# First 224 slots of expert 0 multiplied while the last tokens are routed, and a shorter routing in batches of 8, 7, 3, 3 and 3 rounds

## Chip, core and metric

The kernel runs on one core of one Trainium2 chip. TensorE (PE) multiplies, VectorE (DVE), ScalarE (ACT) and GpSimd (POOL) do the elementwise work, and SyncE (SP) issues most DMAs. The metric is the device time of one execution in microseconds, the median of several. All tensors in memory are float32.

## What is computed

Three blocks follow each other: a gated linear attention, a mixture of experts in which each token goes to one expert, and a gated two-matrix block.

```python
def _attn_ref(q, k, v, f_logit):            # (4, 8, 768, 48)
    f = 1.0 / (1.0 + np.exp(-f_logit))
    for t in range(S):
        state = f[:, :, t, :, None] * state + np.einsum('bhd,bhe->bhde', k[:, :, t], v[:, :, t])
        y[:, :, t] = np.einsum('bhd,bhde->bhe', q[:, :, t], state)

def _moe_ref(x, expert_emb, tau, w1, w2):   # x (3072, 384), 8 experts, w1 (8, 384, 1024)
    logits = xn @ en.T / tau                # xn, en: rows divided by norm + 1e-6
    expert_idx = np.argmax(logits, axis=1)
    probs = softmax(logits)
    for e in range(E):
        mask = expert_idx == e
        h = np.maximum(x[mask] @ w1[e], 0.0)
        out[mask] = probs[mask, e, None] * (h @ w2[e])

def _moe2_ref(x, w_a, w_b, w_out):          # 384 -> 1536 -> 384
    return ((x @ w_a) * (x @ w_b)) @ w_out
```

## The kernel before

**Attention.** 24 rounds `g`, each of 128 tokens of one batch entry and all heads. In a round DVE makes two scans for the decays (`scan_b` of round g+2 at line 190, `scan_r` at line 201) and the products around them, PE the scores, the products with v and the state, ACT the evacuations, POOL the scaled keys `kt` and one causal mask. `turn_y` gives the 128 tokens in PSUM as x together with their logits. Everything is recorded in a fixed order, and each engine works its queue in that order.

**Routing.** Rounds are routed in batches that end at the rounds in `ROUNDS`: 7, 6, 5, 4 and 2 rounds. `route` is a generator whose steps `tick` puts between the rounds: DVE finds each token's expert (`oh`), PE counts ranks (`rk`, on `ones` and `tri`), ACT makes a tanh, DVE the position `posi` and the gate. POOL makes the norm (`nrm`, line 360). `scatter_row` then sends one round's 128 rows by an indirect DMA of POOL to `slots` in memory, at expert times 3072 plus rank. A row is 4 words (token id, gate) and 384 values.

**Weights.** A piece is half of an expert's w1 or w2, 768 KB. It is loaded to one of two `raw` buffers (`w_load`, `job_load`), ACT copies the high part (`w_hi`, line 104, or line 707), and DVE and POOL subtract the low part (`w_lo`, line 112, or line 710). Each product is then three matmuls: high by high, low by high, high by low (`mm3`, lines 810 to 812). Pieces 0 and 1 are made during the attention, 2 and 3 behind the routing.

**Experts.** 64 steps `s`, eight for each expert. Each expert has 448 slots (`CAP`). `rows_load(e)` loads them, `rows_gate` scales them, `x_turn` transposes them and splits them. A step does nine matmuls of w1 (`h_part`), the relu and its split (`h_split`, lines 832 and 833), converts waiting pieces (`w_more`), and does nine matmuls of w2 for the step before (`y_part`, line 863). At expert 0 the rows of expert 2 are asked for in step 6 and scaled in step 8, ahead of the evacuation of expert 0's output on ACT (line 881). `w_more` converts pieces 4 and 5 in step 1 and pieces 6 and 7 in step 5; the loads of the next pieces are issued behind that, as the buffers come free. SP works its loads in order.

**Between the two.** After the last round the queue of DVE holds the rest of the routing, then some fifteen small instructions that make the offsets and a flag (lines 640 to 655; the flag chooses a slow general path when an expert got more than 448 or fewer than 256 tokens), and then the first work on expert 0's rows. PE runs 24 matmuls on zeros there (`warm_up`).

**Last block.** Six tiles of 512 tokens by 12 steps, whose output rows are sent by an indirect DMA.

Of the kernel before, what the change touches and what calls it, by code (L numbers as in the profile page):

```python
# [21 lines left out]
HP = 112  # L22
# [20 lines left out]
ROUNDS = (6, 12, 17, 21, 23)  # L43
C0 = 2.0 ** -15
NWARM3 = 24


def build(tc, I, out, dbg=None):
# [19 lines left out]
    idx = const.tile([128, NT // 128], I32, name="idx")  # L68

# [47 lines left out]
    with tc.manual_schedule():  # L117
# [5 lines left out]
        x_p = actx.enter_context(tc.tile_pool(name="x", bufs=3))  # L123
# [192 lines left out]
        def rounds():  # L316
            return dict(lg=r_p.tile([128, RB, NE], F32, tag="lg", name="lg"),
                        ssq=r_p.tile([128, RB], F32, tag="ssq", name="ssq"),
                        xb=x_p.tile([128, RB, RW], F32, tag="xb", name="xb"), n=0)
# [15 lines left out]
        def x_lg(g):  # L335
# [4 lines left out]
            if g in ROUNDS:  # L340
                bg.append(route(rd))

# [4 lines left out]
        def route(rd):  # L347
            nb = rd["n"]
            lg, ssq = rd["lg"][:, 0:nb], rd["ssq"][:, 0:nb]
            rt = lambda nm, w=NE, dt=F32: r_p.tile([128, RB, w], dt, tag=nm, name=nm)[:, 0:nb]  # L350
# [9 lines left out]
            G.tensor_tensor(out=nrm[:, :, 0], in0=ssq, in1=half[:, 0:nb], op=ALU.pow)  # L360
            yield
# [3 lines left out]
            eq = rt("eq")  # L365
            V.tensor_tensor(out=eq, in0=lg, in1=bc(mx), op=ALU.is_ge)
            yield
# [3 lines left out]
            V.tensor_tensor(out=eq, in0=eq, in1=prio_b, op=ALU.mult)  # L371
# [6 lines left out]
            yield  # L378
            V.tensor_scalar(out=nrm, in0=nrm, scalar1=1e-6, scalar2=None, op0=ALU.add)
# [10 lines left out]
            for i in range(nb - 1):  # L390
                T.matmul(out=ps[:, i + 1:nb], lhsT=ones,
                         rhs=oh[:, i:i + 1].to_broadcast([128, nb - 1 - i, NE]),
                         start=False, stop=(i == nb - 2), skip_group_check=True)
            A.activation(out=z, in_=z, func=ACTF.Tanh, scale=0.5)
            yield
# [4 lines left out]
            pos = rt("pos", 1)  # L400
            V.tensor_reduce(out=pos, in_=pz, axis=AX.X, op=ALU.add)
            yield
            posi = r_p.tile([128, RB, 1], I32, tag="posi", name="posi", bufs=4)[:, 0:nb]
            V.tensor_copy(posi, pos)
# [8 lines left out]
            gate = rt("gate", 1)  # L413
            V.tensor_reduce(out=gate, in_=den, axis=AX.X, op=ALU.add)
            yield
            V.tensor_scalar(out=gate, in0=gate, scalar1=1e-9, scalar2=None, op0=ALU.add)
            yield
            V.reciprocal(out=rd["xb"][:, 0:nb, 1:2], in_=gate)
# [10 lines left out]
        def scatter_row():  # L429
            if scaled:  # L430
# [6 lines left out]
                scat.append(sc)  # L437

# [107 lines left out]
        rd = rounds()  # L546
        for g in range(NG):
# [7 lines left out]
            if g in (2, 12, 14):  # L555
                w_load()
            scan_b(g + 2)
            scores(g + 1)
            tick(g > 5)
# [15 lines left out]
            evac_y(g)  # L575
            if g > 0:
                turn_y(g - 1)
            for _ in range(2 if g < NG - 2 else 6):
# [6 lines left out]
            if g > 0:  # L585
                x_copy(g - 1, rd)
# [10 lines left out]
            if g == NG - 1:  # L597
                w_lo(V, 1)
                w_load()
            tick(3 if g < 19 else 6)  # L600
# [12 lines left out]
        x_lg(NG - 2)  # L613
# [3 lines left out]
        finish()  # L617
        scatter_row()
        scatter_row()
        last = st[NG - 1]  # L620
        x_lg(NG - 1)
        tick()
        st[NG - 1] = last
        x_copy(NG - 1, dict(rd, n=rd["n"] - 1))
        flush_rows()
        finish()
        flush_rows()
# [7 lines left out]
        fl2 = ob_p.tile([1, 3], F32, name="fl2")  # L635
        pc = ps_r.tile([128, 2, 128], F32, tag="r", name="pc")
# [592 lines left out]
```

## Time and profile before

| | us |
|---|---|
| median of 3 runs (lowest, highest) | 888.29 (887.59, 888.86) |
| the profiled execution | 889.81 |
| its span, first to last instruction | 888.0 |
| TensorE busy in the span | 837.8 (94%) |
| VectorE busy | 426.0 (48%) |
| ScalarE busy | 352.9 (40%) |
| GpSimd busy | 245.4 (28%) |

The shares are averages over stages that differ: the attention up to about 147 us, the rest of the routing and the way to the first expert up to about 174 us, the experts up to about 410 us, and the last block. A term that depends on a stage is read from that stretch.

### The profile page before, as it was taken

The page shows a single profiled execution, that of the slowest core. Times are in us where ns is not written, and L with a number is a line of the kernel's source. Part 1 is how long each engine was busy: PE and PEld are TensorE (multiplying, and loading weights), DVE is VectorE, ACT ScalarE, POOL GpSimd, SP SyncE. Part 2 cuts the span into 40 slices and gives each one's busy share as a digit, 9 for nine tenths or more (in the row PEclk, how much of TensorE's full clock was granted, in tenths as well). Part 3 has the DMA queues.
Part 4 walks back from the last instruction along what each step waited for, and adds up shares of the span by engine and source line. Part 5 has one row for each costly group of instructions (what it writes and reads, how often), then busy time and mean ns, then how long its engine had stood idle before and what let it go on. Part 6 is the DMA issues. An engine that isn't in the chain of part 4 may idle for free. (4 is left out here: it accounts for less than half of the span.)

```text
span 888.0 us, 12718 instructions
## 1 busy us (share of the span) xinstructions
PE 837.8 (94%) x5027; PEld 735.4 (83%) x5028; DVE 426.0 (48%) x710; ACT 352.9 (40%) x663; POOL 245.4 (28%) x230
## 2 busy tenths in 40 slices
PE   6899885598999999999998999999999999999996
PEld 4788774397999999999887888888888888888885
DVE  8999996534354445438688423122221312222221
ACT  4798873254455545533444212122221212222111
POOL 6453767433543463441222010010010001001001
PEclk8899998699999999999999999999999999999998
DMA  9898843433634453452233000000000000000001
GB/s 194 193 218 206 224 113 126 157 103 102 198 125 142 165 173 108 140 177 72 72 111 104 1 36 1 1 36 1 0 36 1 1 1 36 0 1 36 1 1 38
DMA packets 36598, 76.58 MB, mean 86 GB/s; under 512 B 4492, under 2 KB 18660, under 8 KB 36532
## 3 DMA queue, kind: packets, MB, share of 16 engines
q1 hardware_dynamic: 33332, 65.91, 26.8%
q0 software_dynamic: 3072, 9.49, 2.9%
q8 instruction: 41, 0.67, 0.3%
q10 hardware_dynamic: 128, 0.30, 0.1%
q14 instruction: 25, 0.20, 0.1%
HBM read 63.79 MB, written 11.90 MB: 85 GB/s over the span
## 5 line engine op out<-in xcount | busy, mean ns | idle before, releaser
L811 PE MATMUL pa<-a,w 128*128 128x512 f32 (+1 forms) x438 | 170.8, 390 | 0.0
L812 PE MATMUL pa<-a,w 128*128 128x512 f32 (+1 forms) x438 | 170.8, 390 | 0.0
L810 PE MATMUL pa<-a,w 128*128 128x512 f32 (+1 forms) x438 | 169.5, 387 | 0.0
L966 DVE TENSOR_TENSOR rows<-rows,pa 128x512 f32<-128x512 f32 (+1 forms) x73 | 49.6, 680 | 242.6 <-PE pa L812 242.6
L993 POOL DMA_INDIRECT out<-yT,idx x24 | 23.4, 975 | 363.8 <-ACT yT L991 358.3
L962 ACT ACTIVATE rows<-pa 128x512 f32<-128x512 f32 (+1 forms) x73 | 43.1, 591 | 164.7 <-PE pa L812 164.4
L967 ACT ACTIVATE gh<-rows 128x512 fp32r<-128x512 f32 (+1 forms) x73 | 45.6, 625 | 143.9 <-DVE rows L966 143.9
L710 POOL TENSOR_TENSOR w<-raw,w 128x512 fp32r<-128x512 f32 x56 | 84.7, 1533 | 62.0 <-ACT w L707 62.0
L981 PE MATMUL pq<-w,gl 128*128 128x384 f32 x288 | 97.8, 340 | 2.1 <-DVE gl L968 2.0
L979 PE MATMUL pq<-w,gh 128*128 128x384 f32 x288 | 97.2, 338 | 1.2 <-ACT gh L967 1.2
L980 PE MATMUL pq<-w,gh 128*128 128x384 f32 x288 | 96.9, 337 | 0.0
L812 PEld LDWEIGHTS pa<-a,w 128*128 128x128 f32 x438 | 82.5, 188 | 16.9
L811 PEld LDWEIGHTS pa<-a,w 128*128 128x128 f32 x438 | 82.5, 188 | 15.4
L810 PEld LDWEIGHTS pa<-a,w 128*128 128x128 f32 x438 | 82.6, 189 | 15.2
L863 PE MATMUL po<-hh,w 128*128 128x448 f32 x384 | 91.4, 372 | 2.4 <-ACT yT L881 2.3
L968 DVE TENSOR_TENSOR gl<-rows,gh 128x512 fp32r<-128x512 f32 (+1 forms) x73 | 60.1, 823 | 52.1 <-ACT gh L967 52.1
L832 ACT ACTIVATE hh<-ph 128x448 fp32r<-128x448 f32 x64 | 34.9, 546 | 113.3 <-PE ph L812 113.3
L863 PEld LDWEIGHTS po<-hh,w 128*128 128x128 f32 x384 | 70.4, 188 | 9.2 <-ACT yT L881 2.9
L833 DVE SCALAR_TENSOR_TENSOR hl<-ph,hh 128x448 fp32r<-128x448 f32 x64 | 39.9, 623 | 79.0 <-ACT hh L832 78.7
L728 POOL TENSOR_TENSOR w<-raw,w 128x768 fp32r<-128x768 f32 x18 | 33.9, 1881 | 142.3 <-ACT w L727 142.3
L810 PE MATMUL ph<-a,w 128*128 128x448 f32 x192 | 71.5, 372 | 0.0
L811 PE MATMUL ph<-a,w 128*128 128x448 f32 x192 | 71.1, 371 | 0.0
(174 smaller groups left out, 1381.6 us busy)
## 6 DMA issues: line engine op xcount, KB each, us to landing
raw<-moe_w SPq DMA_DIRECT2D x32, 768.0 KB, 4.5
qkf<-qkf SPq DMA_DIRECT2D x44, 288.0 KB, 6.2
rows<-slots SPq DMA_DIRECT2D x7, 679.0 KB, 6.5
vx<-vx SPq DMA_DIRECT2D x24, 192.0 KB, 4.8
raw<-moe_w_a SPq DMA_DIRECT2D x6, 768.0 KB, 4.3
raw<-moe_w_b SPq DMA_DIRECT2D x6, 768.0 KB, 4.5
raw<-moe_w_out SPq DMA_DIRECT2D x6, 768.0 KB, 4.5
slots<-raw SPq DMA_DIRECT2D x8, 291.0 KB, 5.1
```

The lines of the kernel that those rows point to most:

```text
L710: (G if i < NPOOL else V).tensor_tensor(out=wt[:, 1, f], in0=raw[:, f], in1=wt[:, 0, f].bitcast(F32), op=ALU.subtract)
L810: T.matmul(out=out, lhsT=wh, rhs=xh, start=first, stop=False)
L811: T.matmul(out=out, lhsT=wl, rhs=xh, start=False, stop=False)
L812: T.matmul(out=out, lhsT=wh, rhs=xl, start=False, stop=last)
L863: T.matmul(out=OS[e][k], lhsT=w[:, j % 4, k * 128:(k + 1) * 128], rhs=x, start=(j == 0 and w is wh and x is hh), stop=(j == FJ - 1 and x i ...
L962: A.activation(out=ab[:, r], in_=pa, func=ACTF.Copy)
L966: V.tensor_tensor(out=ab[:, r], in0=ab[:, r], in1=pp[1], op=ALU.mult)
L967: A.activation(out=gh[:, r], in_=ab[:, r], func=ACTF.Copy)
L968: V.tensor_tensor(out=gl[:, r], in0=ab[:, r], in1=gh[:, r].bitcast(F32), op=ALU.subtract)
L979: T.matmul(out=q, lhsT=gh[:, c], rhs=wh[:, f % 4], start=(f == 0), stop=False)
L980: T.matmul(out=q, lhsT=gh[:, c], rhs=wl[:, f % 4], start=False, stop=False)
L981: T.matmul(out=q, lhsT=gl[:, c], rhs=wh[:, f % 4], start=False, stop=(f == F2J - 1))
```

## The change

Expert 0's first 224 slots (`EN`) are loaded once the first 18 rounds have been scattered, and multiplied through both weight matrices while the last rounds are routed; the 224 other slots follow afterwards in the old place, as steps of 224 columns. The batches of the routing are 8, 7, 3, 3 and 3 rounds, a batch takes 15 DVE instructions in place of 20, and the reciprocal of the gate is taken where the rows are read. Each batch's rows have a buffer of their own. Pieces 2 and 3 are loaded in rounds 13 and 19; piece 2 and two thirds of piece 1's low part go into the rounds, piece 3 behind them. The matmuls on zeros are dropped. The flag is also raised if fewer than 224 rows of expert 0 had arrived at the early load.

```diff
-ROUNDS = (6, 12, 17, 21, 23)
+ROUNDS = (7, 14, 17, 20, 23)
+EN = 224
...
             nrm = rt("nrm", 1)
             G.tensor_tensor(out=nrm[:, :, 0], in0=ssq, in1=half[:, 0:nb], op=ALU.pow)
+            G.tensor_scalar(out=nrm, in0=nrm, scalar1=1e-6, scalar2=None, op0=ALU.add)
...
+        def early_load():
+            V.tensor_copy(run_e, run)
+            ld = SP.dma_start(out=rows[0:HP, 0:2], in_=slots[0:EN].rearrange("(p j) w -> p j w", j=2)).ins
...
+        def early_gate():
+            V.tensor_scalar(out=rg[:, 0:2], in0=rows[0:HP, 0:2, 1], scalar1=1e-9, scalar2=None, op0=ALU.add)
+            V.reciprocal(out=rg[:, 0:2], in_=rg[:, 0:2])
+            V.tensor_copy(ids0, rows[0:HP, 0:2, 0])
+            for j in range(2):
+                r = rows[0:HP, j, XO:RW]
+                A.activation(out=r, in_=r, func=ACTF.Copy, scale=rg[:, j:j + 1])
+
+        def early_turn():
...
+                for j in range(2):
+                    T.transpose(pt[:, j * HP:(j + 1) * HP], rows[0:HP, j, XO + k * 128:XO + (k + 1) * 128],
+                                ident[:HP, :HP])
...
+                A.activation(out=cols(XE[0]), in_=src, func=ACTF.Copy)
+                V.tensor_tensor(out=cols(XE[1]), in0=src, in1=cols(XE[0]).bitcast(F32), op=ALU.subtract)
+
+        def early_h(j):
...
+            for k in range(KC):
+                for i, (w, x) in enumerate(((wh, XE[0]), (wl, XE[0]), (wh, XE[1]))):
+                    T.matmul(out=ph, lhsT=w[:, k, c], rhs=x[:, k], start=(k == 0 and i == 0), stop=(k == KC - 1 and i == 2))
+
+        def early_split(j):
+            hh, hl = HE[j % 2]
+            A.activation(out=hh, in_=EP[j], func=ACTF.Relu)
+            V.scalar_tensor_tensor(out=hl, in0=EP[j], scalar=0.0, in1=hh.bitcast(F32), op0=ALU.max, op1=ALU.subtract)
+
+        def early_y(j):
...
+            for i, (w, x) in enumerate(((wh, hh), (wl, hh), (wh, hl))):
+                for k in range(KC):
+                    T.matmul(out=EP["o"][k], lhsT=w[:, j % 4, k * 128:(k + 1) * 128], rhs=x,
...
-            if g in (2, 12, 14):
+            if g in (2, 12, 13, 19):
                 w_load()
+            if g == 21:
+                early_load()
...
+            if g == NG - 1:
+                early_turn()
...
-            if g in (4, 5, 6, 14, 15, 16):
+            if g in (4, 5, 6, 13, 14, 15, 20, 21, 22):
                 w_hi(1)
-            if g in (5, 6, 7):
+            if g in (5, 6, 7, 14, 15, 18, 23):
                 w_lo(V, 1)
-            if g == NG - 2:
+            if g == 22:
+                early_gate()
                 w_lo(V, 2)
...
-        warm_up(NWARM3)
+        T.matmul(out=pc[0:1, 0, NE:2 * NE], lhsT=ones[:, 0:1], rhs=run_e, start=True, stop=True)
+        early_h(6)
+        early_split(6)
+        early_y(5)
+        early_h(7)
+        early_split(7)
+        early_y(6)
+        early_y(7)
+        early_out()
         V.tensor_copy(cnt_sb, pc[0:1, 0, 0:NE])
...
+        def n_of(e):
+            return CAP - EN if e == 0 else CAP
...
+            if j == late:
+                rows_rate(e + 1)
```

**Order on DVE, rounds 22 and 23.** Before, between the last mask product (`pm`) and the next batch of the routing (`mx`, `eq`); `w_65` is piece 1.

```order
L261 TENSOR_TENSOR pm_2011<-pp,mask 128x512
L112 TENSOR_TENSOR w_65<-raw,w_65 128x1024
L414 TENSOR_REDUCE gate<-den 128x5
L416 TENSOR_SCALAR gate<-gate 128x5
L418 RECIPROCAL xb<-gate 128x5
L423 TENSOR_REDUCE new<-oh 128x8
L425 TENSOR_TENSOR run<-run,new 128x8
L337 TENSOR_REDUCE lg<-x_ps 128x8
```

Now, at the same place; `rg` is the rate made from the rows of the early load, `w_66` piece 2, `oh` the choice on which PE counts.

```order
L268 TENSOR_TENSOR pm_2050<-pp,mask 128x512
L455 TENSOR_SCALAR rg<-rows 112x2
L456 RECIPROCAL rg<-rg 112x2
L457 COPY ids_85<-rows 112x2
L119 TENSOR_TENSOR w_66<-raw,w_66 128x1024
L377 TENSOR_REDUCE mx<-lg 128x3
L380 TENSOR_TENSOR z<-lg,mx 128x24
L383 SCALAR_TENSOR_TENSOR eq<-z,prio 128x24
L386 TENSOR_REDUCE m_2088<-eq 128x3
L389 TENSOR_TENSOR oh<-eq,m_2088 128x24
```

Three instructions that read the early rows stand ahead of the fourth batch's routing on DVE.

**Order on POOL, the last two batches.** Before, from the fourth batch's norm on.

```order
L360 TENSOR_TENSOR nrm<-ssq,half 128x4
L432 DMA slots<-xb,posi 24576x388 x2
L360 TENSOR_TENSOR nrm<-ssq,half 128x2
L332 IOTA xb 128x4
L432 DMA slots<-xb,posi 24576x388 x4
L631 IOTA off_f 1x8 x2
L112 TENSOR_TENSOR w_66<-raw,w_66 128x512
```

Now, from the same norm on; `eo` is the early output.

```order
L435 DMA slots<-xb_1778,posi 24576x388 x3
L373 TENSOR_TENSOR nrm<-ssq,half 128x3
L374 TENSOR_SCALAR nrm<-nrm 128x3
L344 IOTA xb_2031 128x4 x2
L435 DMA slots<-xb_2031,posi 24576x388 x3
L731 IOTA off_f 1x8 x2
L1013 COPY yT_2434<-eo 128x224
```

All three scatters of the fourth batch stand ahead of the fifth batch's norm, where two stood, and the low parts of pieces 2 and 3 have left the queue.

## Rows read from the trace of the kernel before

**Rows 1.** The page: its first line.

```profile
span 888.0 us, 12718 instructions
```

**Rows 2.** Busy time by stretch: us, engines' busy time (instructions), granted clock, DMA share, GB/s.

```profile
32.00:132.80 100.80, 94.83 (x1263) 82.65 (x1259) 98.66 (x181) 89.13 (x236) 58.00 (x67) 1.00 0.82 197
...
147.60:173.60 26.00, 9.52 (x41) 4.39 (x40) 13.56 (x54) 4.23 (x6) 13.61 (x17) 0.64 0.42 141
173.60:181.00 7.40, 6.53 (x24) 5.16 (x22) 1.84 (x3) 1.63 (x3) 0.00 (x0) 0.64 0.38 134
181.00:214.40 33.40, 31.08 (x157) 28.22 (x157) 11.83 (x19) 15.67 (x24) 11.98 (x8) 1.00 0.44 136
```

**Rows 3.** Timeline of DVE in the rounds: start, us, line, operation, tiles, shapes.

```profile
64.61 0.20 DVE L363 TENSOR_REDUCE mx<-lg 128x7 f32<-128x56 f32 x1
...
132.43 0.19 DVE L381 RECIPROCAL nrm<-nrm 128x5 f32<-128x5 f32 x1
132.66 0.20 DVE L383 TENSOR_TENSOR z<-z,nrm 128x40 f32<-128x40 f32 x1
132.77 1.23 DVE L190 TENSOR_TENSOR_SCAN Bt<-F,pat 128x516 f32<-128x516 f32 x1
...
142.92 0.68 DVE L112 TENSOR_TENSOR w<-raw,w 128x512 fp32r<-128x512 f32 x1
143.52 0.18 DVE L363 TENSOR_REDUCE mx<-lg 128x4 f32<-128x32 f32 x1
```

**Rows 4.** Timeline behind the rounds, POOL and DVE; in brackets idle time and what ended it.

```profile
150.00 1.06 POOL L360 TENSOR_TENSOR nrm<-ssq,half 128x4 f32<-128x4 f32 x1
...
161.26 0.98 POOL L432 DMA_INDIRECT slots<-xb,posi  x1 [0.30 <-issue]
...
162.39 2.53 DVE L645 TENSOR_TENSOR off_f<-off_f 1x8 f32<-1x8 f32 x1 [1.06 <-POOL off_f L631]
162.42 2.48 POOL L112 TENSOR_TENSOR w<-raw,w 128x512 fp32r<-128x512 f32 x2
```

**Rows 5.** Line 432, the scatters from 100 to 170 us: start to landing.

```profile
DMA to landing us min/median/max: 2.6/3.4/6.4
```

**Rows 6.** Timeline of SP's queue: rows of experts 0, 1 and 2, pieces 6 and 7.

```profile
167.29 1.96 SPq L770 DMA_DIRECT2D rows<-slots  x3
...
181.86 0.33 SPq L770 DMA_DIRECT2D rows<-slots  x1
...
186.53 2.90 SPq L701 DMA_DIRECT2D raw<-moe_w  x2
...
204.88 0.42 SPq L770 DMA_DIRECT2D rows<-slots  x1
```

**Rows 7.** Timeline of PE: the first matmul of expert 0 and the tenth.

```profile
173.62 0.72 PE L810 MATMUL ph<-a,w 128*128 128x448 f32 x1
...
178.97 0.38 PE L810 MATMUL ph<-a,w 128*128 128x448 f32 x1
```

**Rows 8.** Timeline of ACT: relus of steps 0 and 1, pieces, rows of experts 1 and 2.

```profile
180.45 1.10 ACT L832 ACTIVATE hh<-ph 128x448 fp32r<-128x448 f32 x2 [2.96 <-PE ph L812]
181.45 2.85 ACT L707 ACTIVATE w<-raw 128x1536 fp32r<-128x1536 f32 x2
...
186.31 1.12 ACT L779 ACTIVATE rows<-rows 112x384 f32<-112x384 f32 x2 [0.75 <-DMA rows<-slots]
...
212.03 1.12 ACT L779 ACTIVATE rows<-rows 112x384 f32<-112x384 f32 x2 [3.25 <-DMA rows<-slots]
```

**Rows 9.** Timeline of POOL: the low parts of pieces 4 and 5.

```profile
183.06 5.96 POOL L710 TENSOR_TENSOR w<-raw,w 128x512 fp32r<-128x512 f32 x4 [10.18 <-ACT w L707]
```

**Rows 10.** Timeline of PE: the second matmul on expert 1's output.

```profile
214.40 1.52 PE L863 MATMUL po<-hh,w 128*128 128x448 f32 x5 [2.28 <-ACT yT L881]
```

**Rows 11.** Timeline of PE at the end of the span, the only matmuls of 256 columns.

```profile
875.16 0.28 PE L811 MATMUL pa<-a,w 128*128 128x256 f32 x1
...
875.28 0.28 PE L812 MATMUL pa<-a,w 128*128 128x256 f32 x1
```

More of the change, by code (lines that the diff above doesn't have):

```diff
@@ L68, in build @@
     idx = const.tile([128, NT // 128], I32, name="idx")
+    epool = ctx.enter_context(tc.tile_pool(name="early", bufs=1))
+    rows = epool.tile([128, 4, RW], F32, name="rows")
+    rg = epool.tile([HP, 4], F32, name="rg")
+    ids0 = epool.tile([HP, 2], F32, name="ids0")
+    eo = epool.tile([128, KC, EN], F32, name="eo")
     pieces = []
@@ L341, in x_lg @@
                 bg.append(route(rd))
+                next(bg[-1])
         scat = []
@@ L399, in route @@
             yield
[L400 to L404, printed above, removed]
+            posi = r_p.tile([128, RB, 1], I32, tag="posi", name="posi", bufs=5)[:, 0:nb]
+            with nc.allow_low_precision(reason="whole numbers below 2**24"):
+                V.tensor_reduce(out=posi, in_=pz, axis=AX.X, op=ALU.add)
             yield
@@ L412, in route @@
             yield
[L413 to L418, printed above, removed]
+            V.tensor_reduce(out=rd["xb"][:, 0:nb, 1:2], in_=den, axis=AX.X, op=ALU.add)
             for i in range(nb):
@@ L437, in scatter_row @@
                 scat.append(sc)
+        XE = [ob_p.tile([128, KC, EN], F32R, name=f"xe{i}") for i in range(2)]
+        HE = [[ob_p.tile([128, EN], F32R, name=f"he{i}{n}") for n in range(2)] for i in range(2)]
+        run_e = ob_p.tile([128, NE], BF16, name="run_e")
+        EP = {}
+        def early_load():
+            V.tensor_copy(run_e, run)
+            ld = SP.dma_start(out=rows[0:HP, 0:2], in_=slots[0:EN].rearrange("(p j) w -> p j w", j=2)).ins
+            for sc in scat:
+                tc.add_manual_dep(ld, sc.name, mybir.DependencyInfo(
+                    mybir.DependencyClass.Sync, mybir.DependencyReason.DATA), reason="rows arrived")
@@ new lines, in early_y @@
+        def early_y(j):
+            if j == 0:
+                kv = ps_k.tile([128, 512], F32, tag="kv", name="kv")
+                pq = ps_p.tile([128, 512], F32, tag="pp", name="pq")
+                EP["o"] = [kv[:, 0:EN], kv[:, EN:2 * EN], pq[:, 0:EN]]
+            wh, wl = w_get(2 * (j // 4) + 1, 4)
+            hh, hl = HE[j % 2]
+            for i, (w, x) in enumerate(((wh, hh), (wl, hh), (wh, hl))):
+                for k in range(KC):
+                    T.matmul(out=EP["o"][k], lhsT=w[:, j % 4, k * 128:(k + 1) * 128], rhs=x,
+                             start=(j == 0 and i == 0 and k != 1), stop=(j == FJ - 1 and i == 2), skip_group_check=True)
@@ L439, in finish, with early_out @@
+        def early_out():
+            for k in range(KC):
+                if k == 1:
+                    V.tensor_copy(eo[:, k], EP["o"][k])
+                else:
+                    A.activation(out=eo[:, k], in_=EP["o"][k], func=ACTF.Copy)
         def finish():
@@ L575, in build @@
             evac_y(g)
+            if g == NG - 1:
+                early_turn()
+            if fresh:
+                tick()
             if g > 0:
                 turn_y(g - 1)
-            for _ in range(2 if g < NG - 2 else 6):
+            for _ in range(2 if g < 18 else 3):
                 scatter_row()
@@ L616, in build @@
         rd["n"] += 1
[L617 to L620, printed above, removed]
+        early_h(0)
+        x2 = [st[NG - 2], st[NG - 1]]
+        x_lg(NG - 2)
         x_lg(NG - 1)
[L622 to L627, printed above, removed]
+        tick(5)
+        early_split(0)
+        early_h(1)
+        for i in range(2):
+            st[NG - 2 + i] = x2[i]
+            x_copy(NG - 2 + i, dict(rd, n=1 + i))
+        tick(2)
+        it[0] = NG
+        tick(1)
+        early_split(1)
+        early_y(0)
+        tick(1)
+        early_h(2)
+        tick(2)
+        early_split(2)
+        early_y(1)
+        early_h(3)
+        tick(4)
+        for _ in range(3):
+            scatter_row()
+        tick(3)
+        early_split(3)
+        w_hi(3)
+        early_y(2)
+        early_h(4)
+        early_split(4)
+        w_lo(V, 3)
+        early_y(3)
+        early_h(5)
         off_f = ob_p.tile([1, 4, NE], F32, name="off_f")
```

121 lines of the change are left out of this document (72 added, 49 removed).

## Prediction

> **What bounds the kernel now.** The first line of the page gives a span of 888.0 us [rows 1] in an execution of 889.81 us, so 1.8 us lie around the span; the median of the three runs, 888.29, is 1.5 us under that execution. I add differences to the median.
>
> I read the busy time by stretch first [rows 2]. In the rounds DVE is busy 98.66 of 100.80 us: they are DVE-bound, and every instruction put on DVE there lengthens them. From 147.6 to 173.6 PE is busy 9.5 of 26 us and nobody is full: a chain of latencies. From 181.0 to 214.4 PE is busy 31.1 of 33.4, with one gap of 2.28 us at the end [rows 10]. Behind it PE hardly stops. So the sum needs three pieces: the rounds, the way to the first matmul of the late half of expert 0, and the way from there to the second matmul on expert 1's output at 214.40 [rows 10], behind which both kernels run alike.
>
> I count from the scan of the last round, at 132.77 [rows 3]. On this axis the old kernel reaches its first expert matmul at +40.85 [rows 7], the second relu at +48.2 (the middle of the pair at 180.45, 181.0) and the restart at +81.6 [rows 8, 10].
>
> **The rounds: +2.3 us.** Three thirds of a low part come ahead of that scan, each 0.60 us from its start to the next start (142.92 to 143.52 [rows 3]): +1.8. Of the routing, 49 old instructions lie ahead of it, the first at 64.61 and the last at 132.66 [rows 3]; their spacings sum to 8.9 us. The new kernel has three whole batches there, 45 instructions in unbroken chains. Spacings are 0.23 where one waits for the one before and 0.11 where it doesn't (132.43, 132.66, 132.77 [rows 3]), with 0.3 to 0.5 for a wide reciprocal: 3.2 + 3.2 + 2.9, and 0.2 for the copy of the counts, 9.5. So +0.6, and +2.3 to 2.4 in all. Bounds: +1 if half of it finds idle time, +3.5 if POOL's third scatter in a round holds DVE up.
>
> **The way to the late half: +5.1 us at the first matmul.** Steps counted from the scan:
>
> 1. The third batch's last scatter. POOL spaces scatters by 0.98 + 0.30 = 1.28 us [rows 4]; with three in each of the last rounds its queue is about 0.5 us late, so the last starts near +2.6 and lands 3.4 later, the median [rows 5].
> 2. The early load. Expert 1's 679 KB took from 181.86 [rows 6] to 186.31 [rows 8], 4.45 us; for half of that I put 3.9. It lands at +10.0. DVE has had nothing to do since about +6.5, because `rg` (L455) stands ahead of the fourth batch's routing: a new wait of 3.5 us. Behind it on DVE are a low part, the whole fourth batch and the split of the rows; PE waits for `oh` of that batch, and the last round's inter and intra products stand behind those counts in PE's queue. Nothing is behind the load on SP but the late rows and pieces 4 and 5, which are not yet due.
> 3. Three small instructions, 1.2 us of low part and five of the routing: `oh` at +12.8. Counts and the last round's products 2.2 us, and 0.8 for a slow clock after PE's 4 us of idling: +15.8. Transposes, evacuations and splits of the early rows 1.9, a low part 0.6, the rest of the batch 1.2: gates at +19.5.
> 4. POOL: three scatters, 3.84, then the fifth norm, which took 1.06 for four columns [rows 4] (0.95 for three, and 0.2 for the sum): +24.6. DVE stands at the reciprocal of that norm, and the split of the second early step is behind it: +25.4.
> 5. From there PE is fed. It has twelve groups of nine matmuls left and 0.7 us of counts, less the 0.7 of the group it had begun. Matmuls of 256 columns are 0.12 us apart [rows 11], the nearest row to 224; I put 0.117, 1.05 a group. Early work ends at +38.2.
> 6. The last rows' scatter would start at +29.7 and the late rows land near +37: covered, with 4 us to spare, since DVE reads them only behind the early output and the flag. That is 0.35 for the output, fifteen small instructions at 0.15, and a lock of about 1.0: in the old kernel a DVE instruction of 8 elements took 2.53 us while POOL subtracted for 2.48 [rows 4], and POOL's three copies of the early output now run right there. Rate 0.45, scaling 0.5, transposes 0.45, one copy 0.35: the first matmul at +43.6, 178.7 with the 2.3 of the rounds, against 173.62.
>
> The shorter routing therefore buys nothing at this point: before, SP loaded the rows at 167.29 [rows 6]; now PE's early work and DVE's queue end last, not the rows.
>
> **The late half: -8.0, then +2.3.** From the first matmul to the second relu the old kernel took 7.4 us, much of it at the low clock (mean granted 0.64 in that stretch [rows 2], first matmul 0.72 us, tenth 0.38 [rows 7]). 18 matmuls of 224 columns at that clock and the transposes take 4.2: -3.2.
>
> Then the eight steps, which looks like the prize: 16 groups at 1.05 are 16.8 us where the old took 29.8. But from the second relu on a chain of weights sets the pace, and it doesn't shrink with the columns. Pieces 4 and 5 are converted in step 1 (2.85 us on ACT [rows 8], 5.96 on POOL [rows 9]); 6 and 7 are loaded as POOL frees the buffers, 5.1 us behind (181.45 to 186.53 [rows 6, 8]). The relu of step 5 comes at +10.7 from the second relu, held up by expert 1's rows in steps 2 and 3; pieces 6 and 7 are converted then; POOL needs 6 us; the load of the next pieces and, behind them in SP's queue, of expert 2's rows goes out at +18.7. These rows took 7.15 us (204.88 [rows 6] to 212.03 [rows 8]), behind two pieces of 768 KB: +25.9. The new rate on DVE takes 0.4, and from rows to restart the old kernel took 2.4 (212.03 to 214.40 [rows 8, 10]): +28.65, where the old kernel needed 33.4. So -4.75 and not -13.
>
> PE will have nothing to do for about 7 us there, where it had 2.28. The old kernel kept the full clock over 2.28 us (granted 1.00 [rows 2]), and came at half of it out of the idle stretch ahead of 173.62, for 5.35 us [rows 7]. A little under half of such a time is lost: +2.3.
>
> **The sum.** +5.1 - 3.2 - 4.75 + 2.3 = -0.55, so 887.7 us. Two pages speak to terms of it. "TensorE: Matmul & The Clock Gate" of the Trainium skill (section Back-to-back issue gap) would have matmuls N / 2.4 + 2.5 ns apart, 95.8 ns here; no row shows 224 columns, the row of 256 says 120 where the rule gives 109, and by the rule early work would end 2.3 us sooner, at 885.4 in the end. "SBUF — State Buffer" (section Who interferes with whom) has a DVE instruction with two SBUF inputs fully blocked by a GpSimd instruction that reads SBUF; the 2.53 us agree, and without the rule the lock drops out, 886.7.
>
> **The rivals.**
>
> *Faster, 883 to 885.9.* Expert 2's rows land after 4.45 us, as expert 1's did, in place of 7.15: -2.7 at the restart, 885.0. For it: the pieces ahead of them are spaced a little wider, 3.0 against 2.5 us. Against it: the same three loads follow each other in the same queue. A clock that stays up gives 2.3 alike, 885.4. And if the chain of weights did not bind at all, PE would run through with neither wait nor slow clock: 12.2 us from there, 878 to 880. The chain's own rows speak against that; I give it 0.06.
>
> *Slower, 890 to 893.* The wait at `rg`. DVE works in order, so each microsecond by which the early rows come later than +10.0 goes through `oh`, the gates, the fifth norm and the early steps to the first late matmul. One scatter took 6.4 us to land [rows 5]: +3.0, 890.7. From +12.4 on it decides for slower. A slow clock during the early groups would add 2.3 in the same place, up to 893.
>
> *It doesn't do what it says.* If fewer than 224 rows of expert 0 had been scattered at the load, the flag would send the kernel down the general path, many times slower. Worked out from the reference's inputs, 286 of the first 18 rounds' tokens go to expert 0, and experts get 352 to 417: under 0.01.
>
> **How the numbers follow.** A measurement of this kernel can tell about 0.2%, 1.8 us, from no change. The forecast, gained in expert 0 and given back ahead of it and at expert 1's rows, within 0.2%: 0.38. Faster, by early rows, clock or chain: 0.34. Slower: 0.28. The forecast's own range is 886.5 to 890.0. The whole range goes from 882.0 (both of the first rival's terms, with a margin) to 893.0; about 0.1 lies under it and 0.08 above.
>
> **What would show it.** The scan of the last round 2.3 us later. DVE idle 3 to 4 us ahead of L455, for a DMA. DVE at the fifth batch's reciprocal (L391), waiting for POOL. The early groups closed up from about +25. Late rows that nobody waits for. The first late matmul (L932) near 178.7, and a gap of 6 to 8 us on PE ahead of expert 1's second output matmul (L989), with expert 2's rows as its cause and a granted clock under 1 behind it. I am wrong in kind if that gap is under 3 us, or if PE has no wait between the last round and expert 1; in size if the early rows land before +8 or after +12.5.

## The result and the profile after

The changed kernel takes 893.16 us, the median of 7 runs (891.21 to 895.70), beside 887.59 for 7 runs of the kernel before on the same chip (885.29 to 890.44). The ratio is 1.0061, with a 95% interval of 1.0039 to 1.0083: slower by 0.6%, just above the end of the predicted range (893.0), where no change had been forecast. The profiled execution is the median one, 893.16, with a span of 891.4 where the old kernel's was 888.0 [rows 1]. So the two profiles differ by 3.4 us, the medians by 5.6, and the interval of the ratio stands for 3.5 to 7.4. The old kernel's profiled execution, 889.81, lay 2.2 us above its median; what makes its other executions shorter no profile here shows. The text below accounts for the 3.4.

The first rounds take up to 2.3 us more in one execution than in another: the eleventh scan Bt (for round 10) starts between 57.88 and 60.13 in the profiles of this study. Places of different kernels are therefore counted from that scan, the **mark** (59.74 before, 59.77 after). From it to the last scan Bt the time repeats well: 73.03 to 73.05 in three profiles with the old rounds, 78.53 to 78.67 in six with the new ones.

| from the mark to | before | after |
|---|---|---|
| scan Bt of the last round | 73.03 | 78.57 |
| first (late) matmul of expert 0 | 113.88 | 122.01 |
| restart at expert 1's second output matmul | 154.66 | 155.52 |
| end of the span | 828.26 | 831.63 |

The windows of the kernel after, with the columns of [rows 2]: the rounds, from the second relu's step to the restart, and the restart with the step behind it.

```profile
32.00:138.34 106.34, 97.81 (x1274) 85.04 (x1271) 103.91 (x180) 90.49 (x239) 68.00 (x76) 0.98 0.79 206
...
186.00:216.00 30.00, 21.70 (x161) 19.90 (x161) 12.02 (x24) 14.73 (x27) 11.91 (x8) 0.96 0.52 152
...
215.29:221.19 5.90, 5.89 (x18) 5.26 (x19) 4.08 (x7) 1.64 (x4) 0.00 (x0) 0.56 0.00 0
```

DVE is as full in the rounds as before (103.91 of 106.34), but needs 5.5 us more, and POOL beside it is busy 68.00 us where it was 58.00 [rows 2]. PE idles 8.3 of 30 us ahead of the restart and comes out of that at a granted clock of 0.56.

DVE's timeline in the kernel after (start, length, line, operation, tiles; in brackets idle time and what ended it). The scan Rt is `scan_r`, Bt is `scan_b`, `pm` the masked scores, and `w<-raw,w` a third of a low part:

```profile
90.68 2.07 DVE L208 TENSOR_TENSOR_SCAN Rt<-F,patr 128x516 f32<-128x516 f32 x1
...
121.31 1.65 DVE L208 TENSOR_TENSOR_SCAN Rt<-F,patr 128x516 f32<-128x516 f32 x1
...
123.60 0.69 DVE L119 TENSOR_TENSOR w<-raw,w 128x512 fp32r<-128x512 f32 x1
...
126.79 2.61 DVE L208 TENSOR_TENSOR_SCAN Rt<-F,patr 128x516 f32<-128x516 f32 x1
...
138.34 1.22 DVE L197 TENSOR_TENSOR_SCAN Bt<-F,pat 128x516 f32<-128x516 f32 x1
...
146.68 0.69 DVE L268 TENSOR_TENSOR pm<-pp,mask 128x512 f32<-128x512 f32 x1 [4.19 <-PE pp L251]
148.93 0.17 DVE L455 TENSOR_SCALAR rg<-rows 112x2 f32<-112x2 f32 x1 [1.56 <-DMA rows<-slots]
...
163.81 0.17 DVE L391 RECIPROCAL nrm<-nrm 128x3 f32<-128x3 f32 x1 [3.38 <-POOL nrm L374]
...
177.70 0.14 DVE L750 COPY cnt_sb<-pc 1x8 f32<-1x8 f32 x1
...
179.77 0.15 DVE L889 TENSOR_SCALAR rg<-rows 112x2 f32<-112x2 f32 x1
```

POOL's, in the rounds: scaled keys (L200), causal mask (L259) and a scatter (L435).

```profile
90.45 1.20 POOL L200 TENSOR_TENSOR kt<-qkf,Bt 128x512 f32<-128x512 f32 x1
91.59 1.58 POOL L259 TENSOR_SCALAR_AFFINE_SELECT pm<-pm 128x512 f32<-128x512 f32 x1
...
121.25 0.63 POOL L259 TENSOR_SCALAR_AFFINE_SELECT pm<-pm 128x512 f32<-128x512 f32 x1
...
127.66 0.65 POOL L259 TENSOR_SCALAR_AFFINE_SELECT pm<-pm 128x512 f32<-128x512 f32 x1
...
142.69 0.97 POOL L435 DMA_INDIRECT slots<-xb,posi  x1 [0.30 <-issue]
143.67 1.20 POOL L200 TENSOR_TENSOR kt<-qkf,Bt 128x512 f32<-128x512 f32 x1
```

Read the two together. The scan Rt takes 1.22 us where it meets none of POOL's instructions. Where it meets an instruction of POOL, it ends 1.1 us after that one: at 92.75, the keys at 91.65; at 122.96, the mask at 121.88; at 129.40, the mask at 128.31. The later POOL is with the keys, the longer the scan, until POOL is so late that the scan starts ahead of the keys: then the scan takes 1.22 (133.89) and the product `qc` behind it 1.50 in place of 0.69. Summed over 13 rounds, from one start to the next, the scans Rt take 23.65 us where they took 21.27. At the end of the rounds the keys of the last round stand behind the third batch's scatters (143.67), and DVE waits 4.19 us for the scores made with them.

PE's timeline in the kernel after: the first late matmul, the restart, and the output matmuls at a later expert boundary.

```profile
181.78 0.55 PE L932 MATMUL ph<-a,w 128*128 128x224 f32 x1
...
215.29 2.23 PE L989 MATMUL po<-hh,w 128*128 128x448 f32 x5 [5.72 <-ACT yT L1007]
...
279.26 1.91 PE L989 MATMUL po<-hh,w 128*128 128x448 f32 x6
```

ACT's: the relu of step 1, and two boundaries between experts.

```profile
186.37 0.36 ACT L955 ACTIVATE hh<-ph 128x224 fp32r<-128x224 f32 x1 [0.28 <-PE ph L934]
...
213.10 1.12 ACT L896 ACTIVATE rows<-rows,rg 112x384 f32<-112x384 f32 x2 [5.97 <-DVE rg L890]
...
277.27 1.12 ACT L896 ACTIVATE rows<-rows,rg 112x384 f32<-112x384 f32 x2 [0.98 <-DVE rg L890]
```

SP's queue: a weight piece, and expert 2's rows behind it.

```profile
205.62 0.37 SPq L811 DMA_DIRECT2D raw<-moe_w  x1
206.09 0.42 SPq L880 DMA_DIRECT2D rows<-slots  x1
```

The restart stands as forecast: rows asked for at 206.09 behind the weights, rate and scaling at 213.10, restart at 215.29. New is the 0.98 us at 277.27. The rate of the next rows has become an instruction of DVE that stands behind the split of the step; ACT waits for it ahead of the evacuation of the finished output, and the six output matmuls behind that take 1.91 us in place of 1.40.

### The profile page after: what moved, and what is told of

Same layout as the page of the kernel before. It is cut to its first block, busy times and chain, and to the rows that moved or that the text cites. A ratio compares the mean times of both kernels' runs of the same rounds, so it can differ in the third digit from the quotient of the medians.

```text
span 891.4 us, 12984 instructions
## 1 busy us (share of the span) xinstructions
PE 840.3 (94%) x5149; PEld 742.5 (83%) x5149; DVE 426.6 (48%) x719; ACT 355.9 (40%) x681; POOL 248.4 (28%) x235
## 5 line engine op out<-in xcount | busy, mean ns | idle before, releaser
L989 PE MATMUL po<-hh,w 128*128 128x448 f32 (+1 forms) x384 | 89.7, 365 | 6.9 <-ACT yT L1007 5.7
L989 PEld LDWEIGHTS po<-hh,w 128*128 128x128 f32 x384 | 68.2, 191 | 15.0 <-ACT yT L1007 9.6
L955 ACT ACTIVATE hh<-ph 128x448 fp32r<-128x448 f32 (+1 forms) x64 | 33.3, 520 | 101.3 <-PE ph L934 101.2
L932 PE MATMUL ph<-a,w 128*128 128x448 f32 (+1 forms) x192 | 69.8, 363 | 0.1
L956 DVE SCALAR_TENSOR_TENSOR hl<-ph,hh 128x448 fp32r<-128x448 f32 (+1 forms) x64 | 38.0, 593 | 66.0 <-ACT hh L955 65.8
L933 PE MATMUL ph<-a,w 128*128 128x448 f32 (+1 forms) x192 | 69.3, 361 | 0.0
```

Source lines behind the costliest of these rows:

```text
L932: T.matmul(out=out, lhsT=wh, rhs=xh, start=first, stop=False)
L933: T.matmul(out=out, lhsT=wl, rhs=xh, start=False, stop=False)
L989: T.matmul(out=OS[e][k], lhsT=w[:, j % 4, k * 128:(k + 1) * 128], rhs=x, start=(j == 0 and w is wh and x is hh), stop=(j == FJ - 1 and x i ...
```

## The experiments

The theory behind them: the rounds got longer, beyond the instructions added on DVE, because DVE's scan waits for POOL, and POOL has more to do; what the way to the late half costs are waits in single queues; what the shorter steps of expert 0 should have given is held back by expert 2's rows behind the weights; and a rate behind a split costs time at every later expert. The rivals are that memory or PE stretches the scans, that PE's own work hides the waits, and that the conversion of the weights, not the rows, sets the restart.

Each kernel is the changed one with one edit, unless it says otherwise. Times are medians; ratios are to the kernel before, timed beside it (888.2, 889.6 and 888.9 us in the three series). The changed kernel itself was timed in the first comparison alone, so an experiment is best set against it by the ratios; its own is 1.0061 (1.0039 to 1.0083).

**rows2_ahead**, the chain of weights; the transposes of expert 1's rows move along:

```diff
...
+            if s == 5:
+                x_turn(1, 1)
+                x_turn(1, 2)
+                ids_copy(1)
+                rows_load(2)
             w_more(s)
-            if late + 2 <= j < late + 5:
+            if late + 2 <= j < late + 5 and s not in (5, 6):
                 x_turn(e + 1, j - late - 2)
...
```

> The changed kernel, with expert 2's rows asked for in step 5 ahead of the next weight pieces (their transposes for expert 1 drawn into step 5), in place of behind the pieces in step 6. Theory (the rows, queued behind the weight loads, set PE's restart): the request leaves near 198 us of the span in place of 206.09, the rows land near 204, the gap of 5.72 us ahead of expert 1's second output matmul (L989) falls under 1 us, the granted clock behind it stays at 1.00, and the time falls by 7 to 8.5 us, from 893.2 to 885 or 886. Rival (the conversion of the weight pieces itself sets the pace): a gap of more than 3 us stays in the same place or opens at the next step that needs a new piece, and the time falls by less than 3 us.

Measured: 885.72 us, ratio 0.9985 (0.9970 to 0.9999). SP, PE and the window behind the restart, in that kernel:

```profile
197.07 0.33 SPq L880 DMA_DIRECT2D rows<-slots  x1
```

```profile
208.37 1.33 PE L990 MATMUL po<-hh,w 128*128 128x448 f32 x5 [0.71 <-ACT yT L1008]
```

```profile
208.37:212.20 3.83, 3.83 (x20) 3.48 (x21) 3.66 (x7) 1.64 (x4) 0.00 (x0) 1.00 0.00 0
```

The gap falls from 5.72 to 0.71, the clock stays at 1.00, the step behind the restart takes 3.83 us in place of 5.90, and the span from the mark falls by 6.8. The ratio is 0.0076 below that of the changed kernel, 6.7 us. The rows behind the weights in SP's queue set the restart, and with the gap the low clock behind it goes, worth 2.07 there: both shown.

**before_rows2**, the same move in the kernel before:

> The kernel before, with the same move as in rows2_ahead: expert 2's rows asked for in step 5 ahead of the weight pieces. Theory (the same chain costs the old kernel its gap of 2.28 us at 211.75 to 214.40 and nothing else, since its clock stays up): the gap vanishes, the time falls by 2 to 2.5 us, from 888.2 to 886. Rival (the gap of the old kernel has another cause): no change.

Measured: 883.77 us, ratio 0.9936 (0.9912 to 0.9960). The gap of 2.28 is gone, but the gain is 5.8, more than twice what was expected. With the gap some 2.9 go; most of the rest lies behind the restart, in the steps of experts 1 to 7. **before_again**, the kernel before once more, was to tell whether that belongs to the execution:

> The kernel before once more, for its profile alone. In its first profile the steps of experts 1 to 7 took 3.72 us, in most profiles of other kernels 3.65, at the same granted clock and with the same matmuls; over some 35 such steps that is 2.5 us. If this is a thing of the execution, this profile shows 3.65 (and a span some 2.5 us shorter, 885.5, apart from the clock of the first rounds, which moves by 1.3 between executions); if it is a thing of the kernel, 3.72 and 888.

Measured: span 887.7. The splits of neighbouring steps (the line numbers differ, the line is the same), first in before_again, then in before_rows2, then in expert 1 of the changed kernel, then in expert 1 of lo_before_scan, a run below that changes the rounds alone:

```profile
292.82 0.62 DVE L833 SCALAR_TENSOR_TENSOR hl<-ph,hh 128x448 fp32r<-128x448 f32 x1 [0.87 <-ACT hh L832]
296.54 0.62 DVE L833 SCALAR_TENSOR_TENSOR hl<-ph,hh 128x448 fp32r<-128x448 f32 x1 [1.65 <-ACT hh L832]
```

```profile
288.93 0.62 DVE L834 SCALAR_TENSOR_TENSOR hl<-ph,hh 128x448 fp32r<-128x448 f32 x1 [0.79 <-ACT hh L833]
292.58 0.62 DVE L834 SCALAR_TENSOR_TENSOR hl<-ph,hh 128x448 fp32r<-128x448 f32 x1 [1.58 <-ACT hh L833]
```

```profile
234.11 0.62 DVE L956 SCALAR_TENSOR_TENSOR hl<-ph,hh 128x448 fp32r<-128x448 f32 x1 [0.80 <-ACT hh L955]
237.76 0.62 DVE L956 SCALAR_TENSOR_TENSOR hl<-ph,hh 128x448 fp32r<-128x448 f32 x1 [1.58 <-ACT hh L955]
```

```profile
233.27 0.62 DVE L958 SCALAR_TENSOR_TENSOR hl<-ph,hh 128x448 fp32r<-128x448 f32 x1 [0.87 <-ACT hh L957]
236.99 0.62 DVE L958 SCALAR_TENSOR_TENSOR hl<-ph,hh 128x448 fp32r<-128x448 f32 x1 [1.66 <-ACT hh L957]
```

3.72 us a step in both profiles of the kernel before, 3.65 in before_rows2, with the same 18 matmuls and a granted clock of 1.00. That the two profiles of one kernel agree speaks for the kernel and against the execution. But the changed kernel and lo_before_scan, whose experts are the same instructions, differ in expert 1 (3.65 and 3.72), and both change from one value to the other between experts. So the instructions of a step don't decide it, one profile of a kernel doesn't tell what the next will show, and what sets it stays open. The changed kernel has 3.65 in most of its steps.

**one_scatter**, POOL in the rounds:

```diff
-            for _ in range(2 if g < 18 else 3):
+            for _ in range(1 if g < 16 else 2 if g < 18 else 3):
                 scatter_row()
```

> The changed kernel, with the first batch's rows scattered one in a round (rounds 11 to 15, two in 16, one in 17) in place of two in each of the rounds 11 to 14. Theory (two scatters make POOL late with the scaled keys of the next round, and the scan Rt of that round waits for POOL): the four scans that took 1.85, 2.07, 2.07 and 1.83 us take 1.65, the products qc behind them 0.69 in place of 0.94, the last round's scan Bt comes 1.5 to 2 us earlier than 138.34 and the time falls by as much, to 891.5. Rival (these scans are stretched by the load of the memory or by PE's reads): they stay at 1.8 to 2.1, and the time stays at 893.

Measured: 891.13 us, ratio 1.0037 (1.0022 to 1.0052). Scans Rt of two of the four rounds, and PE's restart:

```profile
88.97 1.64 DVE L208 TENSOR_TENSOR_SCAN Rt<-F,patr 128x516 f32<-128x516 f32 x1
93.83 1.22 DVE L208 TENSOR_TENSOR_SCAN Rt<-F,patr 128x516 f32<-128x516 f32 x1
```

```profile
213.50 2.23 PE L989 MATMUL po<-hh,w 128*128 128x448 f32 x5 [6.86 <-ACT yT L1007]
```

With the keys on time the four scans take 1.22 to 1.65 us, where they took 1.83 to 2.07: POOL's lateness was what stretched them. But a shorter scan is not yet a shorter round. From the mark on, the scans Rt take 2.9 us less, less than in the kernel before, and the last scan Bt comes only 1.16 us earlier, less than the 1.5 expected. The rest turns up as other waits for POOL and ACT: the products `qc` take 0.6 more, and DVE idles 1.05 more, 0.66 of it here:

```profile
108.38 0.20 DVE L391 RECIPROCAL nrm<-nrm 128x7 f32<-128x7 f32 x1 [0.66 <-POOL nrm L374]
```

The first late matmul comes 1.86 earlier. At the restart only 0.53 of it is left, since the gap there grows to 6.86. The median is 2.0 lower, with intervals of the two ratios that overlap, and the profiled execution is not shorter at all (832.6 from the mark to the end; steps of 3.72 in most of its experts), so that how much reaches the end is not settled by this run.

**lo_before_scan** asks whether other work can fill the scan's wait:

```diff
+            if g in (5, 6, 7, 14, 15, 18):
+                w_lo(V, 1)
             scan_r(g + 2)
...
-            if g in (5, 6, 7, 14, 15, 18, 23):
+            if g == 23:
                 w_lo(V, 1)
```

> The changed kernel, with six thirds of low parts in the rounds (5, 6, 7, 14, 15 and 18) recorded ahead of the scan Rt in place of behind the product qc; they depend on nothing recent, so that no wait comes in with them, as one did in route_before_scan. Theory (the scan waits up to 0.43 us for POOL's keys and mask in a quiet round, more in a late one): the scans behind these thirds take 1.22 us in place of 1.65 to 2.07, and the last scan Bt comes 2 to 3 us earlier against the first rounds; the time falls by as much. Rival (the thirds wait for POOL in the scan's place, since they too read two tiles): they take 1.1 us in place of 0.68, and nothing is gained.

Measured: 893.46 us, ratio 1.0057 (1.0040 to 1.0075): no gain that can be told, and the last scan Bt comes 0.4 us later from the mark. DVE in a round of that kernel, a low part and the scan behind it:

```profile
55.88 1.11 DVE L119 TENSOR_TENSOR w<-raw,w 128x512 fp32r<-128x512 f32 x1
56.92 1.22 DVE L208 TENSOR_TENSOR_SCAN Rt<-F,patr 128x516 f32<-128x516 f32 x1
```

The rival holds. The scan is down to 1.22, and the low part waits in its place, 1.11 for 0.68. Whichever instruction reads two tiles of SBUF first meets POOL and pays; `pm` and the state `S`, which read one of their two inputs from PSUM, keep 0.68 and 0.61 in these rounds. The page "SBUF — State Buffer" of the Trainium skill (section Who interferes with whom) has the one that comes second blocked until the other is through. The ends 1.1 us after POOL's agree; the mask at 127.66 does not, since it took its 0.65 us while the scan begun at 126.79 still waited.

**route_before_scan** put the routing there:

```diff
+            fresh = g - 2 in ROUNDS
+            if bg and g < 22:
+                tick(7 if fresh else 30)
             scan_r(g + 2)
...
-            fresh = g - 2 in ROUNDS
-            if bg:
+            if bg and g >= 22:
                 tick(7 if fresh else 30)
```

> The changed kernel, with the seven or eight routing instructions of a round on DVE put ahead of the scan Rt and behind the product pm, in place of behind the product qc. Theory (the scan waits for POOL's scaled keys and causal mask in every round, so that small DVE work ahead of it costs nothing up to 0.43 us in a quiet round and up to 1.4 us in one where POOL is late): the scans of the routing rounds take 1.22 us in place of 1.65 and 2.61, the last scan Bt comes 2 to 3 us earlier against the first rounds than in the changed kernel (78.57 us behind the scan that starts at 59.77), and the time falls by 2 to 3 us from 893.2. Rival (DVE's small instructions with two inputs wait for POOL themselves, as one of 8 elements did that took 2.53 us): the routing instructions get longer by what the scans get shorter, and the time stays within 1 us.

Measured: 902.84 us, ratio 1.0149 (1.0122 to 1.0175). DVE in that kernel:

```profile
77.31 0.20 DVE L415 TENSOR_SCALAR den<-z 128x64 f32<-128x64 f32 x1 [3.15 <-ACT z L405]
...
78.90 1.22 DVE L208 TENSOR_TENSOR_SCAN Rt<-F,patr 128x516 f32<-128x516 f32 x1
```

The scan is at 1.22, but it now stands behind a wait of 3.15 us for the tanh of the same batch, which ACT does behind this round's y. So this run moves work past a wait, and says nothing on whether other work can fill the scan's wait; that is told by lo_before_scan.

**early_b2**, the waits ahead of oh:

```diff
-            if g == 21:
-                early_load()
...
+            if g == 20:
+                early_load()
...
-            if g in (20, 23):
+            if g == 23:
                 for _ in range(3):
                     scatter_row()
```

> The changed kernel, with the early load asked for behind the first two batches of the routing (241 of the first 15 rounds' tokens go to expert 0, and 224 are wanted), so that the third batch's three scatters no longer stand ahead of the last round's scaled keys on POOL. Theory (DVE's waits of 4.19 us for POOL's keys, by way of the scores, and of 1.56 us for the early rows, lie on the way to the first late matmul): both shrink to under 1 us together, oh of the fourth batch comes 5 us earlier than 151.26, the first late matmul 4 to 5 us earlier than 181.78, and the time falls by 4 to 5 us to 888 or 889. Rival (PE's early groups or POOL's later scatters end last anyway): the waits shrink, but the first late matmul moves by less than 2 us and the time stays above 891.

Measured: 889.70 us, ratio 1.0016 (1.0003 to 1.0029). DVE, then POOL:

```profile
142.61 0.69 DVE L268 TENSOR_TENSOR pm<-pp,mask 128x512 f32<-128x512 f32 x1 [1.21 <-PE pp L251]
143.22 0.16 DVE L455 TENSOR_SCALAR rg<-rows 112x2 f32<-112x2 f32 x1
...
148.86 0.18 DVE L391 RECIPROCAL nrm<-nrm 128x3 f32<-128x3 f32 x1 [3.15 <-POOL nrm L374]
```

```profile
143.36 1.01 POOL L435 DMA_INDIRECT slots<-xb,posi  x1 [2.60 <-DMA rows<-slots]
```

The two waits fall from 5.75 to 1.21 together, and oh comes 4.2 us earlier from the mark. The first late matmul comes 2.8 earlier: a new wait of 3.15 stands at the fourth batch's norm, because scatters that must wait for the early load's reading of slots hold POOL's queue. The outcome lies between theory and rival. **early_b2_pool** takes that wait and the second one at L391 (3.38 in the changed kernel, 3.37 in early_b2) away as well:

> early_b2, and two changes of the order on POOL: the third batch's scatters behind the fourth batch's norm (in early_b2 they waited 2.60 us for the early rows and held that norm, and DVE waited 3.15 us for it), and the fifth batch's norm ahead of the fourth batch's scatters (DVE waited 3.37 us for it). Theory (these two waits lie on the way to the first late matmul): both fall under 0.5 us, the first late matmul comes 3 us earlier against the first rounds than in early_b2, and the time falls from 889.7 to 887. Rival (PE's own work between them hides nearly all of it; the second wait cost PE a gap of 1.13 us only): the waits fall, and the time falls by about 1 us, to 888.5.

Measured: 889.63 us, ratio 1.0008 (0.9988 to 1.0029).

```profile
146.50 0.18 DVE L391 RECIPROCAL nrm<-nrm 128x3 f32<-128x3 f32 x1 [0.16 <-POOL nrm L374]
```

The wait at L391 falls from 3.15 to 0.16 and the other one is gone; the first late matmul comes 1.75 us earlier than in early_b2, the restart 1.1, the end 0.8. The rival is nearer: two waits of 6.5 us together on DVE cost under 2 us at PE.

**flag_in_gaps**:

```diff
         early_split(6)
-        early_y(5)
-        early_h(7)
-        early_split(7)
-        early_y(6)
-        early_y(7)
-        early_out()
         V.tensor_copy(cnt_sb, pc[0:1, 0, 0:NE])
...
+        early_y(5)
+        early_h(7)
+        early_split(7)
         V.tensor_reduce(out=fl2[:, 0:1], in_=cnt_sb, axis=AX.X, op=ALU.max)
...
+        early_y(6)
+        early_y(7)
+        early_out()
...
```

> The changed kernel, with the fifteen small DVE instructions of the offsets and the flag moved from behind the early output into DVE's idle gaps between the last early splits. Theory (these 2.1 us, 177.70 to 179.84, lie on the way from the last early matmul to the first late one): the rate of the late rows (L889) follows the early output at once, the first late matmul (L932) comes 2 us earlier than 181.78 and the time falls by 2 us to about 891. Rival (the landing of the late rows, or POOL's copies of the early output, end last there): the first late matmul moves by less than 0.5 us and the time stays.

Measured: 890.58 us, ratio 1.0034 (1.0017 to 1.0051). PE, then ACT:

```profile
213.47 2.23 PE L989 MATMUL po<-hh,w 128*128 128x448 f32 x5 [6.73 <-ACT yT L1007]
```

```profile
189.67 1.12 ACT L896 ACTIVATE rows<-rows,rg 112x384 f32<-112x384 f32 x2 [3.47 <-DVE rg L890]
```

The first late matmul comes 1.75 us earlier from the mark, as the theory has it. At the restart 0.5 is left: expert 1's rows and the weights' chain do not come earlier by as much, and the gap takes up the rest (6.73). Behind it the clock is back sooner: the next output matmuls follow 5.2 us after the restart, in the changed kernel 6.2. From the mark to the end the profile is 0.65 shorter; the median is 2.6 lower, with intervals of the two ratios that overlap.

**rate_ahead**, the expert boundaries:

```diff
+            late = 2 if e == 0 else 0
+            if j == late and s >= 9:
+                rows_rate(e + 1)
             h_part(s)
-            late = 2 if e == 0 else 0
...
-            if j == late:
+            if j == late and s < 9:
                 rows_rate(e + 1)
```

> The changed kernel, with the rate of the next expert's rows (L889, L890) recorded ahead of the matmuls of step 8e for e = 2 to 6, so that DVE makes it before the split of that step and not behind it. Theory (ACT scales the rows ahead of the evacuation of the finished output, and now waits 0.98 us for a rate that stands behind the split on DVE; the old kernel had no such instruction there): the two steps at each of five expert boundaries, 7.96 us in the changed kernel and 7.44 in the old one, fall back to 7.3 to 7.5, and the time falls by 2.5 us, from 893.2 to 890.7. Rival (the longer boundary belongs to the weights or to PE's rhythm): the two steps stay at 7.96 and the time stays.

Measured: 890.25 us, ratio 1.0016 (0.9999 to 1.0034). ACT and PE at the boundary shown above:

```profile
274.03 1.11 ACT L896 ACTIVATE rows<-rows,rg 112x384 f32<-112x384 f32 x2
```

```profile
277.04 1.38 PE L989 MATMUL po<-hh,w 128*128 128x448 f32 x6
```

ACT's wait is gone, the six matmuls take 1.38, the two steps of a boundary 7.30 in place of 7.96, and from the restart to the end the kernel takes 3.6 us less, 3.3 of it at the boundaries. So the rate behind the split costs 0.65 at each of five boundaries of this kernel: shown.

**all_moves** and **all_moves2** put the pieces together:

> rows2_ahead, flag_in_gaps, one_scatter and early_b2_pool in one kernel. If the four lie one behind the other on the same path, their gains add up: 893.2 less 7.5, 2.6, 2.0 and 3.5 to 5 gives 876 to 878, faster than the kernel before (888.2) by 1.1 to 1.4%. If they overlap (the chain of weights or PE's early groups set the end once the rest is shorter), 879 to 883.

Measured: 878.49 us, ratio 0.9877 (0.9845 to 0.9908). That is 14.7 us by the medians and 16.3 by the ratios, of the 15.6 to 17 of a full sum: within what these times can tell the gains add up.

> all_moves with both of these: the rate of rows ahead of the matmuls from step 8 on, and the six thirds ahead of the scan Rt. If all terms lie on one path: 878.5 less 3.3 (six boundaries at 0.5 and 0.3 of the gap of 0.8 left at step 8) less 2 to 3, so 872 to 874. If the thirds gain nothing: 875.

Measured: 873.81 us, ratio 0.9842 (0.9815 to 0.9869), faster than both kernels by 1.6 and 2.2%; no gap is left at the restart. Against the old kernel with the rows moved alike (before_rows2, 883.77) the early half and all that goes with it is worth 8 us (by the ratios) to 10 (by the medians), once rate, flag and scatters stand elsewhere. Whether the thirds gave anything here can't be told from times of 870.5 to 879.0 us. The last scan Bt comes 1.2 us earlier from the mark than in the changed kernel, as in one_scatter; in all_moves it comes only 0.1 earlier, behind a stretch from 81.7 to 85.1 us with a granted clock of 0.50 and 1.4 us of waits of DVE for ACT and PE.

## Why the prediction was wrong, step by step

| term | forecast | measured |
|---|---|---|
| rounds, up to the last scan Bt | +2.3 | +5.54 |
| from that scan to the first late matmul | +2.75 | +2.59 |
| first matmul to second relu | -3.2 | -2.79 |
| second relu to restart | -4.75 | -4.48 |
| clock behind the restart | +2.3 | +2.06 |
| behind that | 0 | +0.45 |
| sum | -0.55 | +3.37 |

**The rounds: the term that failed**, 3.2 of the 3.9 us by which the sum is off in the profiles, and outside its own bounds. The thirds came out as priced, 0.60 each (123.60 to 124.20). Routing cost +1.0 in place of +0.6: fewer instructions, but all of them now stand where nothing covers them, 0.22 apart; some of the old ones stood ahead of a scan that waited for POOL anyway. The missing piece is the scan itself, +2.4, and the product `qc` behind it, +0.5. The prediction named the mechanism as a bound ("+3.5 if POOL's third scatter in a round holds DVE up") and took nothing for it. It was in the trace of before, where most scans Rt of these rounds take 1.55 to 1.85 us and one takes 1.22, with the wait on the product behind it:

```profile
94.91 1.58 DVE L201 TENSOR_TENSOR_SCAN Rt<-F,patr 128x516 f32<-128x516 f32 x1
...
100.18 1.22 DVE L201 TENSOR_TENSOR_SCAN Rt<-F,patr 128x516 f32<-128x516 f32 x1
101.44 1.50 DVE L209 TENSOR_TENSOR qc<-qkf,Rt 128x512 f32<-128x512 f32 x1
```

I read the long ones as the cost of a scan and not as 1.22 and a wait. one_scatter and lo_before_scan show that it is a wait, and also that a wait taken from the scan largely comes back elsewhere in the round.

**The way to the late half: right in sum, partly by luck.** The first late matmul came 43.44 us behind the scan, 43.6 forecast, with early rows at +10.6 (+10.0). But DVE's idle time ahead of L455 was 1.56 and not 3.5, because a wait of 4.19 for POOL's keys, which the prediction did not have, came first and ran beside the transfer. The wait at L391 was there (3.38), late rows were covered, and PE closed up the early groups, at 1.01 each (1.05 forecast). The 0.117 a matmul in that term was 0.112, between the row of 256 columns and the 95.8 ns by the rule that the prediction took from "TensorE: Matmul & The Clock Gate" of the Trainium skill; that page gives it for a matmul by itself, and says that in a stream the spacing of short ones is wider. The lock of 1.0 us at the flag did not occur: POOL's copies ran from 179.98 on, behind the flag's instructions.

**The chain of weights: right.** Restart 28.9 us behind the second relu (28.65), gap 5.72 (6 to 8, so a little under), clock under 1 behind it, price 2.06 (2.3). The rival "the rows land after 4.45 us" did not come: they were asked for at 206.09 and scaled at 213.10. Of the 13 us by which eight shorter steps could have brought the restart forward, 4.5 came; a good part of the rest stood in the gap, since rows2_ahead, with the rows alone asked for earlier, gets 6.8 back at the end.

**Behind the restart both kernels do not run alike**, as the prediction had it. The changed kernel loses 0.5 at each of five boundaries (7.96 against 7.44), +2.6, for an instruction that the diff shows (rows_rate behind h_part) and that I costed at nothing; it wins some 1.8 us by steps of 3.65 in place of 3.72, and 0.4 in the last block. The two sides nearly cancel in the profiles, which is luck: the prediction had neither.

**The slower rival** had the right side and nearly the right time (890 to 893), but by another mechanism: the early rows came at +10.6, far from the +12.4 at which it would have decided.

**What stays open.** The +3.4 of the profiles, added to the median that the prediction started from, would make 891.7, inside the stated range. The measured 893.16 lies outside, since the old kernel's profiled execution was itself 1.5 us above that median, and 2.2 above the median of seven; what makes the difference is not known. One sum of the first rival doesn't come out either: 878 to 880 follows from a gap of 7 us and a clock price of 2.3, but not from the 12.2 us named beside it.

## What to carry to other kernels

A long instruction of DVE that reads two tiles of SBUF while POOL works on others can hold a bare time and a wait: take the shortest row of its kind as the bare time, look at the instruction behind it as well, and ask of every instruction that is added to POOL's queue what it does to the rest. Work put ahead of such a wait doesn't fill it if it reads two tiles too. Work that is moved behind a queue of loads or behind a split keeps that queue's pace, however short it is made itself; before shortening a step, see which request ahead of it is issued too late. Two added instructions of 0.2 us each are not free when another engine waits for them at each turn of a loop.

## What had not been expected of the hardware

The same 18 matmuls of 448 columns take 3.72 us a step in two profiles of the kernel before and 3.65 in before_rows2, at a granted clock of 1.00 and without idle time, for as long as some 35 steps; the changed kernel, lo_before_scan and others have both, and change between experts. A causal mask on POOL, which reads one tile, takes 0.63 us alone and 1.58 when it meets the scan, so that the wait goes both ways.
